# Putting the product of t3 in front of the product of t2 in ten feed-forward pairs of an adaLN + S4 convolution + squared-ReLU kernel

## The chip, the cores and the metric

The kernel runs on one core of a Trainium2 chip. The metric is the device time of one execution in microseconds (us), the median of several runs. Five engines matter here: TensorE (PE in the profile, with its weight loads on a row of their own, PEld), VectorE (DVE), ScalarE (ACT), GpSimd (POOL) and SyncE (SP), which issues nearly all DMAs.

## The reference, cut to what matters

```
mod = (_silu(c) @ w_mod).reshape(c.shape[0], 6, 1, -1)
sa, ca, ga, sb, cb, gb = (mod[:, 0], mod[:, 1], mod[:, 2], mod[:, 3], mod[:, 4], mod[:, 5])
h = _layernorm(x, axis=-1) * (1 + ca) + sa
x = x + ga * _A_ref(h, ...)              # long convolution over 2048 positions, 512 channels
h = _layernorm(x, axis=-1) * (1 + cb) + sb
x = x + gb * _B_ref(h, ...)

def _B_ref(x, w1, b1, w2, b2):           # x 2048 x 512, w1 512 x 1792, w2 1792 x 512
    h = jnp.einsum("bsd,df->bsf", x, w1) + b1
    zero = jnp.zeros_like(h)
    r = jnp.where(h > zero, h, zero)
    h = r * r
    out = jnp.einsum("bsf,fd->bsd", h, w2) + b2
    return out
```

Everything is float32. The change lies in the first product of the feed-forward part, `x @ w1`.

## The kernel before

The first half of the execution (to about 318 us of the span) generates the convolution's kernel and applies it. The feed-forward part fills the rest. It works on the 2048 positions as four blocks of 512, two at a time: `k` is 0 and then 2, and one round computes the blocks `k` and `k + 1`. The 1792 hidden features are 14 tiles of 128, two at a time: a **pair** `j` (0 to 6) makes the tiles `2j` and `2j + 1` for both blocks.

A pair would need eight products of halves (two blocks, two tiles, two halves of the 512 channels). A scheme of the Strassen kind makes them from seven, on sums and differences of the operands. `three(bank, dst, wi, op, start, stop)` is one of them: six matmuls of 128x512 in a row, since weights and operand are each split into a high and a low part (high by high, low by high, high by low, for two groups of 128 channels). `start=True` overwrites the PSUM bank, `start=False` adds to what is in it.

The order of a pair is written out by hand, in `first_half` and `second_half`. From the third pair on (`j` from 2) the banks are `a = tb[0]`, `b = tb[1]`, `c = tb[2]` and `e = tb[3]`; the instruction lists call them ps_163, ps_164, ps_165 and kg_313, and the profile, which leaves numbers out, ps for the first three and kg for the fourth.

1. `"11"` into `a`, overwriting. ScalarE copies `a` to `c0` (line 1184).
2. `"21"` into `b`, overwriting. VectorE adds `b` to `c0` (line 1186). ScalarE and VectorE make the squared ReLU of it (lines 1160, 1165, 1166, 1167), split into high and low, in the buffer t2t.
3. `"t2"` into `a`, **adding**. TensorE may write the bank only once the copy of line 1184 has read it. ScalarE copies the sum to `c1` (line 1194).
4. `"t3"` into `c`, overwriting. VectorE makes `c3 = c1 + c` (line 1196).
5. `"t1"` into `e`, overwriting. VectorE adds `e` to `c3` (line 1198), ScalarE squares it (lines 1160, 1162).
6. 24 matmuls of the second product (`ffn2`, lines 1215 to 1217) for two earlier tiles, into the banks tg. The first twelve take the tile `2j - 1` and the last twelve the tile `2j`, whose squares step 2 has just made.
7. `"t4"` into `c`, adding; VectorE makes `c2 = c1 + c` (line 1203). `"22"` into `e`, adding; VectorE adds it to `c1` (line 1206). Both are squared.

So a pair is 7 x 6 + 24 = 66 matmuls. Between the pairs stand the preparation of weights (`w1_set`: casts on ScalarE and differences on VectorE, lines 1009, 1010 and 1036 to 1039), loads, and on VectorE the residual sums, the statistics of the second normalisation and the output (lines 1113, 1226, 1231, 1244, 1311).

`keep_order` then lays a fixed order on every engine. It plans with costs of its own and a table of numbers, but all matmuls that were put `in_turn` (those of `three` and of `ffn2`) keep the order in which the code issues them. Each engine takes its list strictly in turn, and the waits between engines are semaphores.

Of the kernel before, what the change touches and what calls it, by code (L numbers as in the profile page):

```python
# [358 lines left out]
def tile_adaln_ssm_ffn(  # L359
# [728 lines left out]
    def turn(pe):  # L1088
        in_turn.update(x.ins.name for x in pe)
# [69 lines left out]
    def squares(k, t, c, src=None):  # L1159
        nc.scalar.activation(c, c if src is None else src, AF.Relu, bias=b1c[:, t : t + 1])  # L1160
        if k % 2:
            nc.scalar.activation(rst[:, t], c, AF.Square)
        else:
            h, l = r2_slot(k, t)
            nc.scalar.activation(h, c, AF.Square)
            nc.scalar.activation(c, c, AF.Square)
            nc.vector.tensor_sub(l, c, h.bitcast(F32))  # L1167

    def three(ps, dst, wi, op, start, stop, on=False):
        o = ops[op]  # L1170
        pe = []
        for kt in range(2):
            pe.append(nc.tensor.matmul(  # L1173
                ps, dst[:, 0, wi, kt], o[:, 0, kt], start=start and kt == 0, stop=False, skip_group_check=on))
            pe.append(nc.tensor.matmul(ps, dst[:, 1, wi, kt], o[:, 0, kt], start=False, stop=False, skip_group_check=on))  # L1175
        for kt in range(2):
            pe.append(nc.tensor.matmul(  # L1177
                ps, dst[:, 0, wi, kt], o[:, 1, kt], start=False, stop=stop and kt == 1, skip_group_check=on))
        turn(pe)
# [9 lines left out]
    def second_half(k, j, a, c, e, between):  # L1189
        dst = sets[j % 2]  # L1190
        c1, c2, c3 = quarters(more[:, 0:2048])[1:]
        t = 2 * j
        three(a, dst, 4, "t2", False, True, True)
        nc.scalar.copy(c1, a)
        three(c, dst, 5, "t3", True, True)
        nc.vector.tensor_add(c3, c1, c)
        three(e, dst, 3, "t1", True, True)
        nc.vector.tensor_add(c3, c3, e)  # L1198
        squares(k + 1, t + 1, c3)
        for n in between:  # L1200
            ffn2(k, n, accs)
        three(c, dst, 2, "t4", False, True, True)
        nc.vector.tensor_add(c2, c1, c)
        squares(k, t + 1, c2)
        three(e, dst, 6, "22", False, True, True)
        nc.vector.tensor_add(c1, c1, e)
        squares(k + 1, t, c1)
# [11 lines left out]
    def ffn2(k, t, to):  # L1219
        n = uses.index((k, t))  # L1220
        w2_ready(n + 2)
        product2(k, t, n, to)
# [55 lines left out]
    for k in (0, 2):  # L1278
# [15 lines left out]
        w1_load(2)  # L1294
        w1_load(3)
        second_half(k, 0, tb[0], tb[1], tb[3], [0, 2])
        for _ in w1_set(2, nc.gpsimd):
            pass
        second_half(k, 1, tb[2], tb[1], tb[3], [1])
        for j in range(2, 7):  # L1300
            if j < 6:
                for _ in w1_set(j + 1):
                    pass
            if j < 5:
                w1_load(j + 2)
            if k == 0 and j in (3, 5):
                ss = range(8, 12) if j == 3 else range(12, 16)
                mark = len(nc.cur_bb.bb.instructions)
                for s in ss:
                    nc.sync.dma_start(xos[s % 4], xt[s])  # L1310
                    nc.vector.tensor_add(x2[:, s], x2[:, s], d4(xos[s % 4]))
                    if s % 2:
                        statistics(s - 1)
                hurry(mark, HURRY[55])
            gate_rows(range(4 * k + 2 * j - 4, 4 * k + min(2 * j - 2, 8)))
            first_half(k, j, tb[0], tb[1], cs_[0])
            second_half(k, j, tb[0], tb[2], tb[3], [2 * j - 1, 2 * j])
# [91 lines left out]
```

## Time and profile before

| | us |
|---|---|
| median of 3 runs | 617.12 (617.1 to 618.1) |
| the profiled execution, its own time | 617.67 |
| its span, first to last instruction | 615.9 |
| first changed product in it (first pair with `j = 2`) | 346.51 |
| last matmul starts | 610.13 |
| first and last pair that the change touches, by the copy of line 1184 | 345.9 and 556.3 |

The granted clock of TensorE over the whole span is 0.989 of full speed, and it is 1.00 in every stretch of the feed-forward part that is shown below. In the rows of the timeline the columns are start, duration, engine, line and operation, output and inputs, shape, count, and in brackets the idle time of that engine just before and the instruction that ended it. A matmul's duration overlaps the next one's: what counts is the distance from start to start.

### The profile page before, as it was taken

How to read it: one execution, taken by the hardware profiler on the slowest of the kernel's cores; microseconds unless marked ns; L12 is line 12 of the kernel's file. 1: busy time of each engine (PE TensorE's matmuls, PEld its weight loads, DVE VectorE, ACT ScalarE, POOL GpSimd, SP SyncE). 2: the span in 40 equal slices, each digit the busy share in tenths (PEclk: the TensorE clock that was granted, in tenths of full speed). 3: DMA queues.
4: the chain of work that ended last, by engine and by line, in shares of the span. 5: the costliest groups of instructions: out<-in, count | busy, mean ns of one | idle time of the engine just before them, and what ended most of it. 6: DMA issues, size and time to landing. Idle time of an engine off the chain costs nothing.

```text
span 615.9 us, 21264 instructions
## 1 busy us (share of the span) xinstructions
PE 562.1 (91%) x9238; PEld 484.3 (79%) x9238; DVE 494.9 (80%) x870; ACT 418.6 (68%) x747; POOL 246.7 (40%) x202
## 2 busy tenths in 40 slices
PE   1347998999999999997799999999999999999996
PEld 1235988899899999996677778888888878888885
DVE  6899978999998999945798998547999976654744
ACT  5688869979967678553576866666766766666540
POOL 5549998999998799280004100000000400000000
PEclk9999999999999999998799999999999999999999
DMA  8916041240404401576008131113521532111431
GB/s 307 403 30 202 9 73 31 44 73 4 71 4 72 71 6 27 125 167 224 3 11 278 40 120 35 34 36 99 192 85 55 167 104 69 35 38 40 144 104 69
DMA packets 33133, 57.02 MB, mean 93 GB/s; under 512 B 5520, under 2 KB 14608, under 8 KB 31888
## 3 DMA queue, kind: packets, MB, share of 16 engines
q1 hardware_dynamic: 32752, 55.53, 31.6%
q8 instruction: 72, 1.18, 0.8%
q14 instruction: 21, 0.17, 0.1%
q10 hardware_dynamic: 288, 0.13, 0.1%
HBM read 43.07 MB, written 4.19 MB: 77 GB/s over the span
## 4 chain that ended last, share of the span: by engine, by line
PE 67%; DVE 14%; ACT 9%; issue 4%; DMA 3%; POOL 2%; SPq 1%; DVEq 0%; ACTq 0%; POOLq 0%
PE ps L749 8%; PE ps L903 8%; PE ps L759 7%; PE kg L884 4%; PE ps L1173 4%; PE ps L1175 4%; PE ps L1177 4%; PE tg L1215 3%; PE tg L1217 3%; PE tg L1216 3%; PE tg L1099 2%; PE ps L1217 2%; PE ps L1216 2%; PE ps L1215 2%; DMA work<-w 2%
## 5 line engine op out<-in xcount | busy, mean ns | idle before, releaser
L1036 POOL TENSOR_TENSOR work<-work 128x256 f32<-128x256 f32 x4 | 3.3, 837 | 196.7 <-DVE t2t L1167 134.3
L1010 DVE TENSOR_TENSOR w2t<-rw,w2t 128x512 fp32r<-128x512 f32 x53 | 37.9, 717 | 38.8 <-ACT w2t L1009 38.5
L759 PE MATMUL ps<-xy,t_sb 128*64 128x64 f32 x2048 | 65.9, 223 | 1.0 <-DVE xy L894 1.0
L759 PEld LDWEIGHTS ps<-xy,t_sb 128*64 128x64 f32 x2048 | 63.4, 138 | 2.4 <-DVE xy L894 1.2
L1009 ACT CAST w2t<-rw 128x512 fp32r<-128x512 f32 x53 | 32.8, 619 | 44.6 <-PE kg L1217 21.7
L903 PE MATMUL ps<-e_sb,xy 128*64 128x128 f32 x1024 | 61.0, 274 | 1.9 <-DVE xy L894 1.2
L903 PEld LDWEIGHTS ps<-e_sb,xy 128*64 128x64 f32 x1024 | 56.3, 139 | 3.1 <-DVE xy L894 1.4
L1160 ACT ACTIVATE more<-more,b1c 128x512 f32<-128x512 f32 x54 | 38.9, 720 | 26.4 <-DVE more L1198 15.9
L1215 PE MATMUL tg<-w2t,t2t 128*128 128x512 f32 x112 | 43.9, 392 | 0.5 <-DVE t2t L1167 0.5
L1216 PE MATMUL tg<-w2t,t2t 128*128 128x512 f32 x112 | 43.6, 389 | 0.0
L1217 PE MATMUL tg<-w2t,t2t 128*128 128x512 f32 x112 | 43.6, 389 | 0.0
L894 DVE TENSOR_TENSOR xy<-ps,xy 128x512 f32<-128x512 f32 x64 | 39.9, 681 | 0.5 <-PE ps L759 0.4
L1009 ACT CAST wset<-work 128x512 fp32r<-128x512 f32 (+2 forms) x36 | 24.6, 690 | 22.1 <-DMA work<-w 13.1
L1173 PE MATMUL ps<-opt,wset 128*128 128x512 f32 x84 | 34.1, 405 | 2.4 <-ACT more L1184 2.4
L840 POOL TENSOR_TENSOR llph<-lo,big 128x1024 int32<-128x1024 int32 x16 | 34.3, 2144 | 3.7 <-ACT tg L852 3.6
L840 POOL TENSOR_TENSOR rtlph<-lo,big 128x1024 int32<-128x1024 int32 x16 | 34.4, 2151 | 3.4 <-ACT tg L852 2.8
L749 PE MATMUL ps<-d_sb,ksb 128*64 128x128 f32 x512 | 33.8, 276 | 2.0 <-ACT tg L850 1.4
L1215 PE MATMUL ps<-w2t,t2t 128*128 128x512 f32 x84 | 33.4, 398 | 0.0
L1217 PE MATMUL ps<-w2t,t2t 128*128 128x512 f32 x84 | 32.8, 391 | 0.0
L1175 PE MATMUL ps<-opt,wset 128*128 128x512 f32 x84 | 32.8, 391 | 0.0
L1216 PE MATMUL ps<-w2t,t2t 128*128 128x512 f32 x84 | 32.7, 390 | 0.0
L749 PE MATMUL ps<-d_sb,big 128*64 128x128 f32 x512 | 32.1, 274 | 0.1
(287 smaller groups left out, 1640.1 us busy)
## 6 DMA issues: line engine op xcount, KB each, us to landing
rw<-w SPq DMA_DIRECT2D x53, 256.0 KB, 2.7
xy<-xy SPq DMA_DIRECT2D x64, 128.0 KB, 4.1
xy<-xt SPq DMA_DIRECT2D x24, 256.0 KB, 5.4
work<-w SPq DMA_DIRECT2D x12, 512.0 KB, 4.3
out_dram<-more SPq DMA_DIRECT2D x14, 256.0 KB, 2.2
xy<-w_mod SPq DMA_DIRECT2D x3, 1024.0 KB, 9.9
xy<-w_mod SPq DMA_DIRECT2D x12, 256.0 KB, 3.5
t_sb<-c_t SPq DMA_DIRECT2D x1, 2048.0 KB, 15.3
```

The costliest lines, as they stand in the source:

```text
L749: nc.tensor.matmul(ps[64 * r : 64 * r + 64, 128 * i : 128 * i + 128], src[:, i], d1_sb[:, r], start=True, stop=True)
L759: nc.tensor.matmul(ps[64 * r : 64 * r + 64, 64 * i : 64 * i + 64].rearrange("p (h q t) -> p q h t", h=2, t=2), t2_sb[:, 8 * g + i, r], src ...
L840: nc.gpsimd.tensor_tensor(ph.rearrange("p d r (a b) -> p (d r) a b", a=4), bc(low_phase[:, us].rearrange("p d r b -> p (d r) b"), 2, 4), b ...
L894: nc.vector.tensor_mul(product_piece(y, g), ps, piece(x, g))
L903: nc.tensor.matmul(ps[64 * m : 64 * m + 64, 128 * i : 128 * i + 128], pairs(y)[:, g, i // 2, 64 * m : 64 * m + 64, i % 2], e1_sb[:, h], st ...
L1009: nc.scalar.copy(hi_, raw_)
L1160: nc.scalar.activation(c, c if src is None else src, AF.Relu, bias=b1c[:, t : t + 1])
L1173: pe.append(nc.tensor.matmul(ps, dst[:, 0, wi, kt], o[:, 0, kt], start=start and kt == 0, stop=False, skip_group_check=on))
L1175: pe.append(nc.tensor.matmul(ps, dst[:, 1, wi, kt], o[:, 0, kt], start=False, stop=False, skip_group_check=on))
L1215: nc.tensor.matmul(to[m], l[:, xs], hi_, start=(t == 0), stop=False),
L1216: nc.tensor.matmul(to[m], h[:, xs], lo_, start=False, stop=False),
L1217: nc.tensor.matmul(to[m], h[:, xs], hi_, start=False, stop=(t == NF - 1))])
```

## The change

For `j` from 2 on, in both rounds, the call for t3 stands in front of the call for t2. For `j` 0 and 1 nothing changes (there `c` is another bank or the code before is another).

```
         c1, c2, c3 = quarters(more[:, 0:2048])[1:]
         t = 2 * j
+        if j > 1:
+            three(c, dst, 5, "t3", True, True)
         three(a, dst, 4, "t2", False, True, True)
         nc.scalar.copy(c1, a)
-        three(c, dst, 5, "t3", True, True)
+        if j < 2:
+            three(c, dst, 5, "t3", True, True)
         nc.vector.tensor_add(c3, c1, c)
```

No instruction is added or removed, on any engine. The lines after the edit move down: the copy of line 1194 is line 1196 in the changed kernel, the adds of lines 1196 and 1198 are 1199 and 1201, and the second product's 1215 to 1217 are 1218 to 1220.

The first place is TensorE's list in the first changed pair (`k = 0`, `j = 2`), right behind the product of `"21"`. ps_163 is the bank `a`, ps_165 the bank `c`, opt_5427 the operand t2 and opt_5426 the operand t3. Before:

```order
L1173 MATMUL ps_163<-opt_5427,wset_4635 128x512
L1175 MATMUL ps_163<-opt_5427,wset_4635 128x512
L1173 MATMUL ps_163<-opt_5427,wset_4635 128x512
L1175 MATMUL ps_163<-opt_5427,wset_4635 128x512
L1177 MATMUL ps_163<-opt_5427,wset_4635 128x512 x2
L1173 MATMUL ps_165<-opt_5426,wset_4635 128x512
L1175 MATMUL ps_165<-opt_5426,wset_4635 128x512
L1173 MATMUL ps_165<-opt_5426,wset_4635 128x512
L1175 MATMUL ps_165<-opt_5426,wset_4635 128x512
L1177 MATMUL ps_165<-opt_5426,wset_4635 128x512 x2
```

The same place in the changed kernel:

```order
L1173 MATMUL ps_165<-opt_5426,wset_4635 128x512
L1175 MATMUL ps_165<-opt_5426,wset_4635 128x512
L1173 MATMUL ps_165<-opt_5426,wset_4635 128x512
L1175 MATMUL ps_165<-opt_5426,wset_4635 128x512
L1177 MATMUL ps_165<-opt_5426,wset_4635 128x512 x2
L1173 MATMUL ps_163<-opt_5427,wset_4635 128x512
L1175 MATMUL ps_163<-opt_5427,wset_4635 128x512
L1173 MATMUL ps_163<-opt_5427,wset_4635 128x512
L1175 MATMUL ps_163<-opt_5427,wset_4635 128x512
L1177 MATMUL ps_163<-opt_5427,wset_4635 128x512 x2
```

Six matmuls have changed places with six others; this is so in the ten pairs with `j` from 2 to 6 in both rounds, and nowhere else on TensorE.

The second place is ScalarE's list in the pair `k = 2`, `j = 2`, around the copy of `a` to `c1`. Before:

```order
L1165 ACTIVATE t2t<-more 128x512
L1166 ACTIVATE more<-more 128x512
L1194 COPY more<-ps_163 128x512
L1009 CAST wset_4635<-work 128x512
L1160 ACTIVATE more<-more,b1c 128x512
```

The same place in the changed kernel:

```order
L1165 ACTIVATE t2t<-more 128x512
L1166 ACTIVATE more<-more 128x512
L1009 CAST wset_4635<-work 128x512
L1196 COPY more<-ps_163 128x512
L1160 ACTIVATE more<-more,b1c 128x512
```

The planner has put one cast of the next weights ahead of the copy, in three pairs (`k = 2`, `j` 2, 3 and 4). On VectorE the add of line 1196 changes places with the instruction behind it in four pairs: with the matching subtraction of line 1010 in those three, and with line 1126 in the pair `k = 0`, `j = 6`. The lists of GpSimd and SyncE are the same.

## The prediction

> **What bounds the kernel now.** I read the page first, then the waits of TensorE in the feed-forward part, then the ten places of the edit one by one.
>
> ```profile
> PE 562.1 (91%) x9238; PEld 484.3 (79%) x9238; DVE 494.9 (80%) x870; ACT 418.6 (68%) x747; POOL 246.7 (40%) x202
> ...
> PE 67%; DVE 14%; ACT 9%; issue 4%; DMA 3%; POOL 2%; SPq 1%; DVEq 0%; ACTq 0%; POOLq 0%
> ```
>
> TensorE is busiest and carries 67% of the chain that ended last. In the stretch that holds all ten edited pairs (338 to 573 us), the list of who waited for whom has one wait of TensorE's matmuls, and for its weight loads the same one on top:
>
> ```profile
> PE ps L1173 <- ACT more L1184: 2.4, 3, 1.0
> ...
> PEld ps L1173 <- ACT more L1184: 5.6, 10, 1.5
> ```
>
> Line 1184 is ScalarE's copy of bank `a` to `c0`, line 1173 a product's first matmul. The product that must wait for this copy is t2, and ten weight loads waited: one in each pair that the change touches. Elsewhere TensorE goes from matmul to matmul in these 235 us, so time saved at these ten places moves what follows forward, as long as nobody else is the bound. The busy time by stretch shows who could be:
>
> ```profile
> 348.00:363.00 15.00, 14.21 (x63) 11.48 (x62) 14.72 (x36) 10.47 (x20) 0.00 (x0) 1.00 0.29 89
> 363.00:378.00 15.00, 15.00 (x67) 12.11 (x66) 13.55 (x25) 9.58 (x17) 0.00 (x0) 1.00 0.31 88
> 378.00:393.00 15.00, 15.00 (x67) 12.19 (x66) 9.72 (x16) 10.92 (x19) 0.00 (x0) 1.00 0.13 36
> 423.00:470.00 47.00, 46.99 (x222) 38.66 (x222) 45.79 (x75) 31.48 (x52) 0.00 (x0) 1.00 0.32 101
> ```
>
> The columns are stretch, length, and busy time of PE, PEld, DVE, ACT and POOL, then the granted clock (1.00), the DMA share and GB/s. From 348 to 363 VectorE is busy 14.72 us of 15, more than TensorE; from 378 it has 5 us of air in 15; from 423 to 470, between the rounds, it has 1.2 us in 47. So the pairs with `j` 2 to 4 of the first round are VectorE's as much as TensorE's, and the rest is TensorE's.
>
> **The change, part by part.** First the size of a product and of each stall. The first matmul of t3 and that of t1, one product later:
>
> ```profile
> 348.00 0.39 PE L1173 MATMUL ps<-opt,wset 128*128 128x512 f32 x1
> 349.36 0.39 PE L1173 MATMUL kg<-opt,wset 128*128 128x512 f32 x1
> ```
>
> Six matmuls take 1.36 us, so the step is 0.227 us. The last two matmuls of `"21"` are the row of line 1177 (x2); undisturbed, t2 starts 0.45 us after it and its second matmul (line 1175) 0.68 us after it. What that second matmul is later than this is the loss of the pair:
>
> ```profile
> 345.30 0.61 PE L1177 MATMUL ps<-op,wset 128*128 128x512 f32 x2
> 346.85 0.40 PE L1175 MATMUL ps<-opt,wset 128*128 128x512 f32 x1
> 361.15 0.61 PE L1177 MATMUL ps<-op,wset 128*128 128x512 f32 x2
> 362.89 0.39 PE L1175 MATMUL ps<-opt,wset 128*128 128x512 f32 x1
> 377.19 0.61 PE L1177 MATMUL ps<-op,wset 128*128 128x512 f32 x2
> 378.13 0.40 PE L1175 MATMUL ps<-opt,wset 128*128 128x512 f32 x1
> 392.44 0.61 PE L1177 MATMUL ps<-op,wset 128*128 128x512 f32 x2
> 393.26 0.40 PE L1175 MATMUL ps<-opt,wset 128*128 128x512 f32 x1
> 494.79 0.61 PE L1177 MATMUL ps<-op,wset 128*128 128x512 f32 x2
> 496.43 0.50 PE L1173 MATMUL ps<-opt,wset 128*128 128x512 f32 x1 [1.03 <-ACT more L1184]
> 496.77 0.40 PE L1175 MATMUL ps<-opt,wset 128*128 128x512 f32 x1
> 541.36 0.61 PE L1177 MATMUL ps<-op,wset 128*128 128x512 f32 x2
> 542.18 0.39 PE L1175 MATMUL ps<-opt,wset 128*128 128x512 f32 x1
> ```
>
> The losses are 0.87 (346.85 less 345.30 less 0.68), 1.06, 0.26 and 0.14 us for `j` 2 to 5 of the first round; 1.30 for `j = 2` of the second, and 0.14 for its `j = 5`, with `j` 3 and 4 alike. In the two pairs with `j = 6` I find 0.03 each and leave them out. The sum is 0.87 + 1.06 + 0.26 + 1.30 + 4 x 0.14 = 4.05 us. That is the ceiling of the gain, since the change removes no matmul.
>
> What remains after the swap hangs on when the copy ends. The copies of the four large stalls:
>
> ```profile
> 345.89 0.57 ACT L1184 COPY more<-ps 128x512 f32<-128x512 f32 x1
> 361.93 0.56 ACT L1184 COPY more<-ps 128x512 f32<-128x512 f32 x1
> 377.18 0.57 ACT L1184 COPY more<-ps 128x512 f32<-128x512 f32 x1
> 495.82 0.56 ACT L1184 COPY more<-ps 128x512 f32<-128x512 f32 x1
> ```
>
> They end at 346.46, 362.49, 377.75 and 496.38. In all four the second matmul of t2 follows 0.38 to 0.40 us after the copy's end, so "copy's end plus 0.39" is the earliest for it. After the change its undisturbed place is one product, 1.36 us, later.
>
> - `k = 0`, `j = 2`: place 345.98 + 1.36 = 347.34; earliest 346.85. No stall; gain 0.87.
> - `j = 3`: TensorE arrives 0.87 earlier, place 361.83 - 0.87 + 1.36 = 362.32. The copy will not come earlier: ScalarE waits in this stretch for VectorE, whose list is full. Earliest 362.88, so 0.56 stays. Gain so far 0.87 + 1.06 - 0.56 = 1.37.
> - `j = 4`: place 377.87 - 1.37 + 1.36 = 377.86, earliest 378.14, 0.28 stays against 0.26 now. Gain so far 1.35.
> - `j = 5`: VectorE and ScalarE have air and follow TensorE's pace, so the copy moves forward too; the 0.14 goes. Gain of the first round 1.49.
> - `k = 2`, `j = 2`: place 495.47 + 1.36 = 496.83, earliest 496.77, if the copy moves forward with TensorE: gain 1.30. With `j` 3 to 5 at 0.14 each the second round gains 1.72.
>
> The sum is 1.49 + 1.72 = 3.2 us.
>
> The edit adds no wait to TensorE where t3 now stands. t3 overwrites bank `c`, which the previous pair's add of line 1203 must have read, and its weights come in the same instruction as those of t2:
>
> ```profile
> 343.22 0.68 DVE L1203 TENSOR_TENSOR more<-more,ps 128x512 f32<-128x512 f32 x1
> ...
> 492.53 0.68 DVE L1203 TENSOR_TENSOR more<-more,ps 128x512 f32<-128x512 f32 x1
> ```
>
> These end at 343.90 and 493.21, and t3 would start at 345.75 and 495.24: 1.85 and 2.0 us to spare. I cost this at nothing; its cover is that room.
>
> It does add a wait to ScalarE: the copy of line 1194 can start one product later, and ScalarE's list stands behind it (a cast of weights, then the squaring of `c3`, line 1160). In the tightest pair, and in the second round where the cast now goes first:
>
> ```profile
> 408.01 0.42 PE L1173 MATMUL ps<-opt,wset 128*128 128x512 f32 x1
> ...
> 411.02 0.57 ACT L1194 COPY more<-ps 128x512 f32<-128x512 f32 x1
> ...
> 413.52 0.72 ACT L1160 ACTIVATE more<-more,b1c 128x512 f32<-128x512 f32 x1 [1.94 <-DVE more L1198]
> 500.18 0.62 ACT L1009 CAST wset<-work 128x512 fp32r<-128x512 f32 x1
> ```
>
> In the pair of 411.02 t2 began at 408.01; as second product it ends near 408.01 + 2 x 1.36 + 0.16 = 410.9 (the last matmul lasts 0.39 and not 0.23), still before the copy. Were it late, 1.94 us of idle time behind would take it up. The cast at 500.18 has no idle time before it, so its data had landed, and moving it forward by the copy's 0.5 us costs nothing that TensorE sees. The add of line 1196 needs the copy as it did, and `"t4"`, which adds to its bank, comes only 30 matmuls after t2. The swaps on VectorE move 0.4 to 0.6 us each between neighbours. All at nothing; a bound for each is 0.6 us where its cover is gone.
>
> What comes late next is the second tile's operand in `ffn2`, the low part that VectorE makes in line 1167. Tightest where TensorE leads most and VectorE not yet follows:
>
> ```profile
> 381.95 0.69 DVE L1167 TENSOR_TENSOR t2t<-more,t2t 128x512 fp32r<-128x512 f32 x1 [0.26 <-ACT more L1166]
> 384.73 0.39 PE L1215 MATMUL tg<-w2t,t2t 128*128 128x512 f32 x1
> ```
>
> It ends at 382.64 and is used at 384.73; with a lead of 1.35 at 383.38, which leaves 0.74 us. Enough, but the thinnest margin of all.
>
> A rule of the Trainium skill is to be weighed here. The row is that of 348 to 363: VectorE 14.72, TensorE 14.21. The page "Perfetto Trace Analysis", section "Identifying the Most-Contended Engine", says that the engine with the highest occupancy is the one to improve first, with occupancy a fair measure for VectorE and matmul busy time a bad one for TensorE. By it VectorE is the bound there, and a swap on TensorE's list gives nothing in that stretch. By the rows it is half right: the copy stays where VectorE puts it, yet TensorE needs it one product later.
>
> **Rivals.**
>
> *VectorE holds the lead down.* Its 45.79 us of 47 between the rounds would not follow TensorE, and the copy at 495.82 would stay at its absolute time. Then all that was gained until there counts against one late copy: its earliest place is 496.77, and TensorE behind t2 and t3 is ahead by one product at most, 1.36 us. With 3 x 0.14 behind it, 1.8 us in all. For it: this list, and an output operation that stretches to 2.56 us shortly before that copy. Against: before 423 VectorE has idle time in each pair and starts on what TensorE gives it. By the page of the Trainium skill named above, this case is the one to come.
>
> ```profile
> 488.59 2.56 DVE L1231 TENSOR_TENSOR more<-more,big 128x512 f32<-128x512 f32 x1
> ```
>
> *The wait only moves.* TensorE, early at `ffn2`, waits for line 1167 instead, by as much as it won. That needs the 0.74 us (and more in the other pairs) to vanish and VectorE to lag in both rounds. Gain near nothing.
>
> *Slower: t3 is held by bank `c`.* If VectorE came to the add of line 1203 later than now by over 1.9 us in every pair, each t3 would wait for it in a place that had no wait. At 2.4 us late it is 0.5 us a pair, 5 us in ten, less the 3.2: 1.8 us slower. For it: VectorE's full list in three pairs; against: in the other seven it has the air that 378 to 393 shows, and its order before line 1203 does not change.
>
> That the change does not do what it says is out: TensorE's list has t3 in front in just these ten pairs.
>
> **How the numbers follow.** The sum stands against the profiled execution: 617.67 - 3.2 = 614.5 us. The median of the runs shown (617.12) lies 0.55 below that execution; on the runs' scale I predict 617.12 - 3.2 = 613.9 us. Its own range goes from the ceiling (617.12 - 4.05 = 613.1) to 615.0, where a third is lost: chance 0.70. VectorE holding the lead gives 617.12 - 1.8 = 615.3: 0.17. The wait that only moves gives 617.1: 0.07. Held by bank `c` gives 618.9: 0.06. The range of 8 in 10 is 612.8 to 616.0: the first two cases, with the runs' scatter of some tenths below. What a measurement of this kernel can tell from no change is about 0.2%, 1.23 us, so faster means below 615.9: 0.70 and most of the 0.17, 0.85; within: 0.02 and 0.07, 0.09; slower 0.06.
>
> **What will show it.** In the profile after, TensorE's waits on the copy of line 1184 should be gone in `k = 2`, `j = 2` (1.03 us as recorded) and in `k = 0`, `j = 2`; 0.3 to 0.6 us should stay in `k = 0`, `j` 3 and 4. Weight loads that wait for it should fall from ten to two or three. The distance from the copy at 345.89 to that of the last pair, now 210.4 us (556.3 less 345.9, from the table), should shrink by 3 us, and the last matmul come 3 us earlier. Wrong would be: a new wait of line 1218 on line 1167, of t3 on line 1206 (the old 1203), or a copy at 495.82 that hasn't moved.

## The result, and the profile after

| | before | changed |
|---|---|---|
| median of 20 runs each | 618.13 us (616.44 to 622.8) | 615.31 us (613.0 to 618.05) |
| ratio of changed to before | | 0.9947, 95% interval 0.9935 to 0.9959 |
| span of the profiled execution | 615.9 us | 613.8 us |

The changed kernel is faster by 0.5%; the ratio gives 3.3 us (2.5 to 4.0), the medians 2.8. The forecast was a gain of 3.2 us and a time of 613.9, the range 612.8 to 616.0.

The page of the changed kernel, the row of engines and the chain that ended last, reads almost as before:

```profile
PE 560.4 (91%) x9238; PEld 483.6 (79%) x9238; DVE 495.1 (81%) x870; ACT 419.6 (68%) x747; POOL 247.0 (40%) x202
...
PE 69%; DVE 14%; ACT 8%; issue 3%; POOL 2%; DMA 2%; SPq 1%; DVEq 0%; ACTq 0%; POOLq 0%
```

The waits tell more. Between 338 and 573 us TensorE's matmuls, and below them its weight loads, waited for others as follows (in total, times, longest):

```profile
PE ps L1173 <- ACT more L1184: 0.8, 1, 0.8
PE tg L1218 <- DVE t2t L1167: 0.2, 1, 0.2
...
PEld ps L1173 <- ACT more L1184: 1.6, 2, 1.2
PEld tg L1218 <- DVE t2t L1167: 1.5, 3, 0.6
```

Before, three matmuls waited 2.4 us and ten weight loads 5.6 us for the copy of line 1184; now it is one matmul and two loads. The wait of line 1218 for 0.2 us is the one at 338.28, ahead of the first edited pair, and it was longer before (0.47). The places, in TensorE's timeline of the changed kernel (t2 is now the product behind t3; the releaser is in brackets):

```profile
347.49 0.61 PE L1177 MATMUL ps<-opt,wset 128*128 128x512 f32 x2
347.95 0.39 PE L1173 MATMUL ps<-opt,wset 128*128 128x512 f32 x1
...
363.86 0.50 PE L1173 MATMUL ps<-opt,wset 128*128 128x512 f32 x1 [0.80 <-ACT more L1184]
364.20 0.40 PE L1175 MATMUL ps<-opt,wset 128*128 128x512 f32 x1
...
378.50 0.61 PE L1177 MATMUL ps<-opt,wset 128*128 128x512 f32 x2
379.12 0.50 PE L1173 MATMUL ps<-opt,wset 128*128 128x512 f32 x1
379.47 0.40 PE L1175 MATMUL ps<-opt,wset 128*128 128x512 f32 x1
...
495.95 0.62 PE L1177 MATMUL ps<-opt,wset 128*128 128x512 f32 x2
496.41 0.39 PE L1173 MATMUL ps<-opt,wset 128*128 128x512 f32 x1
```

In `k = 0`, `j = 2` and in `k = 2`, `j = 2` t2 starts 0.46 us behind the last two matmuls of t3: no loss, where 0.87 and 1.30 us were lost before. In `j = 4` the second matmul is 0.97 behind, 0.29 later than the undisturbed 0.68. In `j = 3` 1.07 us is lost (t2's first matmul 0.96 later than the step of 0.227, its second another 0.11). The other six pairs lose nothing.

What that is worth is best read between two points that both kernels share and that lie around the ten pairs: the first matmul of the second product in the pair `k = 0`, `j = 1`, and one behind the last pair of the second round. First the two of before, then the two of the changed kernel:

```profile
337.46 0.50 PE L1215 MATMUL tg<-w2t,t2t 128*128 128x512 f32 x1 [0.47 <-DVE t2t L1167]
...
572.15 0.50 PE L1215 MATMUL tg<-w2t,t2t 128*128 128x512 f32 x1
```

```profile
338.28 0.50 PE L1218 MATMUL tg<-w2t,t2t 128*128 128x512 f32 x1 [0.18 <-DVE t2t L1167]
...
570.03 0.50 PE L1218 MATMUL tg<-w2t,t2t 128*128 128x512 f32 x1
```

Before, TensorE needs 234.69 us for the distance, now 231.75: **2.94 us less**. The spans differ by only 2.1, because this execution came to the first point 0.82 us later, in work that the edit does not touch. From here on "the distance" is this number, and "lost at t2" is the sum over the ten pairs. (The expectations below call the distance "from the first to the second round's start"; it begins in the first round and ends behind the second.)

### The profile page after: what moved, and what is told of

Same layout as the page of the kernel before. It is cut to its first block, busy times and chain, and to the rows that moved or that the text cites. A ratio compares the mean times of both kernels' runs of the same rounds, so it can differ in the third digit from the quotient of the medians.

```text
span 613.8 us, 21258 instructions
## 1 busy us (share of the span) xinstructions
PE 560.4 (91%) x9238; PEld 483.6 (79%) x9238; DVE 495.1 (81%) x870; ACT 419.6 (68%) x747; POOL 247.0 (40%) x202
## 4 chain that ended last, share of the span: by engine, by line
PE 69%; DVE 14%; ACT 8%; issue 3%; POOL 2%; DMA 2%; SPq 1%; DVEq 0%; ACTq 0%; POOLq 0%
PE ps L903 7%; PE ps L749 7%; PE ps L759 6%; PE ps L1173 4%; PE ps L1175 4%; PE ps L1177 4%; PE tg L1218 4%; PE tg L1220 4%; PE tg L1219 4%; PE kg L884 3%; PE ps L1220 3%; PE ps L1218 3%; PE ps L1219 3%; PE kg L1173 2%; PE kg L1175 2%
```

## The experiments

There were ten runs. In all of them the same instructions are issued; what differs is an order. The planner lays the lists anew each time, so a run that moves something by hand also differs in some places of the lists of ScalarE and VectorE, all of them behind 343 us. In "swap in the first pair alone" the lists of ScalarE, VectorE and GpSimd are those of before, and in the repeats those of the run repeated. Their profiles, beside those of before and of the changed kernel (the last two columns: the time of before in the runs taken with it, and the ratio to it):

| kernel | lost at t2, us | the distance, us | time, us (runs) | before, us | ratio |
|---|---|---|---|---|---|
| before | 4.05 | 234.69 | 618.13 (20) | | |
| changed | 1.36 | 231.75 | 615.31 (20) | 618.13 | 0.9947 (0.9935 to 0.9959) |
| changed, second profile | 0.72 | 231.08 | 614.94 (7) | 618.22 | 0.9932 (0.9907 to 0.9958) |
| changed, third profile | 1.04 | 231.46 | 615.16 (1) | 617.54 | |
| swap in the first pair alone | 4.0 | 234.69 | 618.69 (1) | 618.71 | |
| swap in `k = 2`, `j = 2` alone | 3.0 | 233.62 | 616.27 (1) | 618.71 | |
| t3, t1, then t2 | 0 | 230.60 | 614.03 (6) | 618.71 | 0.9937 (0.9914 to 0.9959) |
| the same, second profile | 0 | 230.60 | 613.78 (12) | 618.22 | 0.9928 (0.9907 to 0.9949) |
| t3 already between "11" and "21" | 0.37, and 0.23 at t3 | 231.66 | 614.47 (5) | 618.71 | 0.9936 (0.9913 to 0.9960) |
| changed, one cast put behind the copy | 0.89 | 231.26 | 614.66 (7) | 618.22 | 0.9926 (0.9899 to 0.9953) |
| before, copy ahead of the squarings | 2.16 | 232.60 | 616.24 (12) | 618.22 | 0.9971 (0.9952 to 0.9990) |
| before, copy ahead of both ReLUs | 0 | 230.36 | 613.10 (6) | 617.54 | 0.9930 (0.9913 to 0.9947) |

**One swap alone, where VectorE's list is full.** The forecast says that the copy in `j = 3` does not come earlier when TensorE does, so a lead won in `j = 2` is lost one pair later. (Not shown here and in the next two runs: the `if` in front of the later call for t3 is changed to match, in the third also one in front of the call for t1.)

```
-        if j > 1:
+        if k == 0 and j == 2:
             three(c, dst, 5, "t3", True, True)
```

> Only the pair k = 0, j = 2 has t3 in front; the other nine stay as before. My theory (in the next pair, j = 3, the copy of bank a is late because VectorE and a load of second weights make it late, not because TensorE is): the stall of 0.87 us at j = 2 goes, but the whole lead is lost at j = 3, whose stall of t2 grows from 1.06 to about 1.9 us (up to 2.4 if the load is as late as in the changed kernel's profile); from j = 4 on nothing is gained, 0 to 0.1 us. Rival (the copy follows TensorE): the stall at j = 3 stays at 1.06 and 0.87 us are gained.

The first loss went, and the next one grew:

```profile
363.64 0.50 PE L1173 MATMUL ps<-opt,wset 128*128 128x512 f32 x1 [1.72 <-ACT more L1184]
```

It is 1.99 us now (1.89 to the first matmul, 0.10 more to the second) where before lost 1.06, so 0.93 came back of the 0.87 won. The copy had not moved: it starts 24.52 us behind the first point, where it started 24.47 behind it before. The distance is 234.69 us, as before. So in these pairs a lead is worth only what the next copy's place allows, and the swap in `j = 3` is what keeps the gain of the one in `j = 2`.

**One swap alone, where VectorE has air.**

```
-        if j > 1:
+        if k == 2 and j == 2:
```

> Only the pair k = 2, j = 2 has t3 in front. My theory: its stall of 1.30 us goes whole, nothing gives it back later, and TensorE's stalls at t2 in the first round are as before (0.87, 1.06, 0.26, 0.14). Counted from the first ffn2 matmul of the second round to the last matmul the kernel is 1.3 us shorter. Rival (the wait only moves): TensorE waits by about as much, 1 us, for the second tile's operand of ffn2 in that pair or the next, and the gain is under 0.3 us.

The loss of 1.30 us in that pair went. The distance can be divided at the matmul that stands in the first round where the second point stands in the second (423.21 before, 423.11 here). Up to it nothing was won: 86.00 us where before took 85.75, since t2 in `j = 3` lost 1.24 instead of 1.06. From there to the second point it took 147.62 us where before took 148.94: 1.32 less. The whole of the 1.30 was kept.

**t2 as the third product.** Two products between "21" and t2, so that the copy has 1.36 us more.

```
-        if j > 1:
+        late = j > 1
+        if late:
             three(c, dst, 5, "t3", True, True)
+            three(e, dst, 3, "t1", True, True)
         three(a, dst, 4, "t2", False, True, True)
```

> In the ten pairs the order is t3, t1, t2, so t2 has two products of room behind the product of 21 and the adds to c3 come after both. My theory: the stalls left in the changed kernel at k = 0, j = 3 and 4 (1.07 and 0.29 us) go too, and the gain over the kernel before is 3.7 to 4.1 us (ratio 0.9933 to 0.9940); what may come up is a wait of ffn2's second tile on the low part of the squares at k = 0, j = 4, 0.1 to 0.5 us, where TensorE now leads by 2.2 us and the room was 2.1. Rival (VectorE is the bound in that stretch): the 1.4 us come back as such waits, and the ratio is that of the changed kernel, 0.9947. Second rival: the copy of c1, two products later now, holds up ScalarE's list and the gain is smaller than the changed kernel's.

No loss at t2 is left. In its place is the thinnest margin of the forecast, line 1167 against the second tile of the second product in `k = 0`, `j = 4` (line 1167's rows of VectorE carry the same number in this kernel, the second product's lines are 1221 to 1223):

```profile
381.53 0.69 DVE L1167 TENSOR_TENSOR t2t<-more,t2t 128x512 fp32r<-128x512 f32 x1 [0.27 <-ACT more L1166]
```

```profile
381.91 0.39 PE L1223 MATMUL tg<-w2t,t2t 128*128 128x512 f32 x1
382.27 0.50 PE L1221 MATMUL tg<-w2t,t2t 128*128 128x512 f32 x1
382.61 0.40 PE L1222 MATMUL tg<-w2t,t2t 128*128 128x512 f32 x1
```

The subtraction ends at 382.22 and the matmul follows at 382.27: 0.25 us lost up to the matmul behind it. So the wait that only moves exists, but it is small, and in this pair it begins only when TensorE has won more than the swap wins. The gain was within the forecast (a ratio of 0.9937, forecast 0.9933 to 0.9940).

**t3 one product earlier.** This takes 1.36 us from the 1.85 that t3 had to spare for bank `c`. (Not shown: the call for t3 in `second_half` goes for these pairs, and `tb[2]` is handed over as `c`.)

```
     three(a, dst, 0, "11", True, True)
     nc.scalar.copy(c0, a)
+    if c is not None:
+        three(c, dst, 5, "t3", True, True)
     three(b, dst, 1, "21", True, True)
```

> In the ten pairs the order is 11, t3, 21, t2, t1: t2 keeps the place that it has in the changed kernel, t3 goes one product earlier still and 21 one later. My theory: the stalls at t2 are those of the changed kernel; bank c, whose room was 1.85 to 2.0 us in the changed kernel, still has about 0.5 us and holds t3 nowhere or by at most 0.3 us a pair; the squares of c0 come one product later, so ffn2's second tile waits for them by about 0.6 us at k = 0, j = 4. Ratio 0.9947 to 0.9965. Rival of the prediction (t3 is held by bank c): t3's first matmul waits for VectorE's add of c2 in most pairs, by 0.3 us or more, and the kernel is no faster than before.

One t3 was held. In `k = 0`, `j = 4` its second matmul starts 0.91 us behind the last two of "11" where 0.68 is undisturbed, so 0.23 us is lost: VectorE's add that reads bank `c` (line 1206 in this kernel) ends only at 376.14.

```profile
375.62 0.61 PE L1177 MATMUL ps<-op,wset 128*128 128x512 f32 x2
376.19 0.50 PE L1173 MATMUL ps<-opt,wset 128*128 128x512 f32 x1
376.53 0.40 PE L1175 MATMUL ps<-opt,wset 128*128 128x512 f32 x1
...
375.46 0.68 DVE L1206 TENSOR_TENSOR more<-more,ps 128x512 f32<-128x512 f32 x1
```

The other nine were not held, so the rival, 0.3 us or more in most pairs, did not come; with 1.36 us less room the bank begins to matter in one pair. t2 lost 0.37 us in `j = 3`. The second product waited for line 1167, 0.55 us, in `k = 2`, `j = 2` and not in `k = 0`, `j = 4` as forecast. The ratio, 0.9936, is better than the 0.9947 to 0.9965 forecast. Here the planner also moved instructions of ScalarE and VectorE and one load of SyncE, so the 231.66 us is not the price of this move alone.

**The load in front of the copy.** In `j = 3` the changed kernel lost 1.07 us where 0.56 was forecast. ScalarE's list there, with the waits in brackets:

```profile
359.83 0.62 ACT L1009 CAST w2t<-rw 128x512 fp32r<-128x512 f32 x1 [1.10 <-DMA rw<-w]
360.36 0.40 ACT L1009 CAST wset<-work 128x256 fp32r<-128x256 f32 x1
360.67 0.72 ACT L1160 ACTIVATE more<-more,b1c 128x512 f32<-128x512 f32 x1
...
363.24 0.57 ACT L1184 COPY more<-ps 128x512 f32<-128x512 f32 x1
```

From the cast of a weight of the second product to the copy ScalarE has no idle time, and the cast waited for its load. The ReLU of line 1160 could have started when VectorE's add of line 1206 was done, at 359.91:

```profile
359.23 0.68 DVE L1206 TENSOR_TENSOR more<-more,ps 128x512 f32<-128x512 f32 x1
```

So the cast was put behind the copy, with this addition to the planner:

```
+    group_of = {i.name: g for g, il in enumerate(groups) for i in il}
+    for x, y in links:
+        before[group_of[y]].add(group_of[x])
...
+[(copied[0, 3], cast_of[7])]
```

> The changed kernel with one thing more: in the pair k = 0, j = 3 ScalarE's cast of a second-product weight (w2t from rw), which in the changed kernel stood three squarings and two casts ahead of the copy of bank a and waited 1.10 us for its load, is put behind that copy. TensorE's list is that of the changed kernel. Theory: the 1.07 us left at t2 in this pair is set by that load, since ScalarE takes its list in turn. Without it the squaring ahead of the copy waits only for VectorE's add, which ended at 359.91 in the changed kernel where the squaring started at 360.67: the copy comes about 0.7 us earlier and 0.3 to 0.4 us is left of 1.07. From the first to the second round's start TensorE needs 231.1 instead of 231.75 us, and the time is 0.4 to 0.7 us below that of the changed kernel. Rival: VectorE sets the copy (14.7 us busy of 15 there), the load only ended the wait last by a little; then 0.8 to 1.1 us stays at t2 and the time is that of the changed kernel.

> The changed kernel once more, for the spread between executions: from the first to the second round's start 231.2 to 232.0 us (231.75 in its first profile), with 0.5 to 1.1 us left at t2 of k = 0, j = 3, by when the load ahead of the copy lands. If the 1.07 us were fixed by VectorE's list it would come out at 1.0 to 1.1 again.

> The changed kernel a third time, one look: what is left at t2 of k = 0, j = 3 follows the landing of the load that ScalarE's cast ahead of the copy needs (1.07 us left where the cast started 0.60 after VectorE's add began, 0.44 where it started 0.16 after it); 231.0 to 231.8 us between the starts of the rounds.

With the cast gone, the ReLU waits for VectorE, and the copy comes 3.29 us after that add's start where it came 4.01 after it (its lines are 6 higher, the add is line 1212, start 359.37):

```profile
360.08 0.73 ACT L1166 ACTIVATE more<-more,b1c 128x512 f32<-128x512 f32 x1 [0.91 <-DVE more L1212]
...
362.66 0.57 ACT L1190 COPY more<-ps 128x512 f32<-128x512 f32 x1
```

0.37 us is left in `j = 3`, as forecast, but 0.52 in `j = 4`: counted from the first point, TensorE came there 0.70 us earlier than in the first profile of the changed kernel and the copy only 0.46 earlier, so 0.2 is given back. The distance, 231.26 us (forecast 231.1), lies within what the changed kernel itself took (231.08 to 231.75), and the times can't tell the two kernels apart either (614.66 and 614.94 on one chip). So this run shows what sets the copy, but no gain. The repeats of the changed kernel say more: the cast, the copy and the same add of VectorE in the second profile, then in the third:

```profile
357.82 0.62 ACT L1009 CAST w2t<-rw 128x512 fp32r<-128x512 f32 x1 [0.66 <-DMA rw<-w]
...
361.23 0.56 ACT L1184 COPY more<-ps 128x512 f32<-128x512 f32 x1
...
357.66 0.68 DVE L1206 TENSOR_TENSOR more<-more,ps 128x512 f32<-128x512 f32 x1
```

```profile
359.19 0.62 ACT L1009 CAST w2t<-rw 128x512 fp32r<-128x512 f32 x1 [0.90 <-DMA rw<-w]
...
362.59 0.56 ACT L1184 COPY more<-ps 128x512 f32<-128x512 f32 x1
...
358.79 0.68 DVE L1206 TENSOR_TENSOR more<-more,ps 128x512 f32<-128x512 f32 x1
```

In all three profiles the copy starts 3.40 or 3.41 us after the cast. After the start of VectorE's add the cast came by 0.16, 0.40 and 0.60 us (second, third and first profile), and 0.44, 0.80 and 1.07 us were lost at t2. Counted from the first point of each execution (in the same order), the add came at 20.78, 20.93 and 20.95 us and the cast at 20.94, 21.33 and 21.55, so the cast moved by 0.61 us, as the loss did (0.63), and the add by 0.17. The load was issued at 17.94, 18.09 and 18.11 and landed 2.9, 3.2 and 3.4 us later. The loss follows the landing of the load: the same lists lose more or less from one execution to the next. Why the load takes longer or shorter is not shown. The second profile's 231.08 us and 0.44 lie just below the 231.2 to 232.0 and 0.5 to 1.1 forecast for it, the third within its range.

**The copy moved instead of the product.** If the wait is the cost, and not the order of products, then TensorE's order of before must do as well once ScalarE copies earlier. Line 1184's copy needs only the product of "11", but it stood behind the previous pair's ReLUs and squarings. First it was put ahead of the squarings:

```
+        links.append((copied, squared[k, 2 * j - 1]))
```

> The kernel before (t2 in front of t3), with ScalarE's list changed instead of TensorE's: the planner must put the copy of bank a (c0) ahead of the two squarings of the previous pair's c2 (lines 1165 and 1166, 0.53 and 0.54 us apart), and rearranges VectorE's, ScalarE's and SyncE's lists around it. Theory: the loss at t2 is the wait for this copy and nothing in the order of products itself, so it goes without the swap: the stalls of 1.30 (k = 2, j = 2) and of the four times 0.14 us go, those of k = 0 shrink; 2 to 3.5 us gained, 614.5 to 616 us. Rival: what the copy gains is given back, since the squares of c2, 1.1 us earlier in the list before, now come late for the second product (line 1215 on line 1167) or VectorE, which is full there, becomes later: the stalls at t2 go, new waits of the second product come, and the time is 617 to 619.

Half of it went: 0.77, 0.11 and 0.48 us are lost in `j` 2 to 4 of the first round and 0.80 in `k = 2`, `j = 2`, where the forecast had the whole 1.30 gone; the time, 616.24, just misses the 614.5 to 616 forecast. The copy was still behind the ReLU of `c1`, and that waits for VectorE's add of the product "22" (line 1213 here):

```profile
347.46 0.72 ACT L1165 ACTIVATE more<-more,b1c 128x512 f32<-128x512 f32 x1 [0.53 <-DVE more L1213]
348.09 0.56 ACT L1189 COPY more<-ps 128x512 f32<-128x512 f32 x1
```

Then it was put ahead of both ReLUs:

```
+        links.extend((copied, relus[x]) for x in ((k, 2 * j - 1), (k + 1, 2 * j - 2)))
```

> The kernel before (t2 in front of t3) with the copy of bank a put ahead of both ReLUs of the previous pair (of c2 and of c1, line 1160), not only ahead of the squarings as in the last try, where it still stood behind the ReLU of c1. ScalarE's copy then needs nothing but the end of the product of "11", which comes about 2.8 us ahead of the second matmul of t2. Theory: the cost is the copy's place in ScalarE's list; all ten losses at t2 go (4.05 us) without any change of TensorE's order, at most 0.5 us of it comes back at the second product (its squares are one copy, about 0.5 us, later); 230.4 to 231.2 us from the first to the second round's start where the kernel before has 234.69, and 3.4 to 4.2 us less time. Rival: losses at t2 go, but the later squares make TensorE wait in the second product (line 1215 on line 1167) or at the next "21" and more than 1.5 us of it come back.

In all ten pairs the copy now waits for TensorE, here in the first pair and in `k = 2`, `j = 2`:

```profile
343.51 0.59 ACT L1189 COPY more<-ps 128x512 f32<-128x512 f32 x1 [1.24 <-PE ps L1182]
...
490.61 0.59 ACT L1189 COPY more<-ps 128x512 f32<-128x512 f32 x1 [0.30 <-PE ps L1182]
```

All ten losses are gone, with t2 in its old place. In the ten pairs neither a matmul nor a weight load waits for the later squares; three weight loads wait 1.4 us for line 1172 (the old 1167), at the first point, between the rounds and at the second point, where those of before and of the changed kernel wait too. The distance, 230.36 us, and the gain in time, 4.4 us, come out slightly better than forecast. Its windows, in the columns of the prediction:

```profile
348.00:363.00 15.00, 15.00 (x68) 12.42 (x67) 14.79 (x34) 11.11 (x21) 0.00 (x0) 1.00 0.30 79
423.00:470.00 47.00, 47.00 (x223) 38.80 (x223) 46.41 (x74) 31.26 (x50) 0.00 (x0) 1.00 0.32 102
```

TensorE is busy 15.00 us of 15 beside a VectorE at 14.79. At 613.10 us this is the fastest kernel measured here, though its interval overlaps those of the changed kernel and of "t3, t1, then t2".

**t2 as the third product, once more.**

> t3, t1 and then t2, once more and on the same chip as the changed kernel. Theory: every loss at t2 is gone here (230.6 us from the first to the second round's start, 1.15 less than in the changed kernel's first profile), so it is about 1 us below the changed kernel's time. Rival: what it wins beyond the changed kernel is within the spread between executions, and the two times agree within 0.5 us.

The distance was 230.60 us again, 0.48 less than the changed kernel's profile on the same chip. Its time was 613.78 us against 614.94 for the changed kernel, 1.2 us less, but the two intervals of the ratio overlap almost wholly, so the times alone don't show it; and about 0.3 of the 1.2 lies outside the span, as the last section says.

## Why the prediction was right

*What bounds the kernel.* Right: the ten places carried the gain. The distance less what is lost at t2 is 230.4 to 230.7 us in eleven of the twelve profiles of the table, whichever way the loss was removed, and 231.3 with t3 between "11" and "21", where 0.23 us was lost at t3 and 0.55 at the second product instead. Matmul by matmul in the second round, the lead of the changed kernel over before grows by 1.35, 0.18, 0.17, 0.18 and 0.06 us in the five pairs and by nothing between them. So each stall cost a little more than its second matmul shows (1.30, 0.14 three times, 0.03), and the ceiling of 4.05 was a little low: the copy ahead of both ReLUs won 4.33.

*The pairs one by one.* Of the 4.05 us, 0.84 was forecast to stay, in `j` 3 and 4. In `j = 4` 0.28 was forecast and 0.29, 0.28 and 0.24 measured. In `j = 3` 0.56 was forecast and 1.07, 0.44 and 0.80 measured, 0.77 in the mean. This is the mis-sized term. The step behind it read "The copy will not come earlier: ScalarE waits in this stretch for VectorE", and took the copy's time from one execution. VectorE is only one of the two for which ScalarE's list waits there; the other is the load of a weight, and it moves the copy by some tenths from one execution to the next. With the cast out of the way VectorE alone left 0.37; the rest is the load. The trace of before had shown it too, as the idle time of ScalarE's cast at 358.53:

```profile
358.53 0.62 ACT L1009 CAST w2t<-rw 128x512 fp32r<-128x512 f32 x1 [0.64 <-DMA rw<-w]
```

*The two rounds.* Forecast were 1.49 and 1.72 us. The three profiles of the changed kernel gained 1.03, 1.69 and 1.31 in the first round, and 1.91, 1.92 and 1.92 in the second (147.02 or 147.03 us where before took 148.94). Both together are 3.26 us in the mean of the three; 3.2 was forecast. That they agree so closely is in part luck: the first round came out 0.15 below its forecast in the mean, by the load, and the second 0.20 above it, by stalls that cost more than was read. The kernel before has only one profile; in the first round, "swap in `k = 2`, `j = 2` alone" has its order and took 0.25 us longer, so the gains of the first round are no surer than that.

*The earliest place of t2.* "Copy's end plus 0.39" held in every pair that was stalled at t2, in all profiles: 363.81 and 364.20 in the changed kernel, 361.79 and 362.18 in its second profile, 348.65 and 349.04 with the copy ahead of the squarings.

*The rival "VectorE holds the lead down".* It fell. Between the rounds VectorE moved with TensorE, at 45.85 us of 47 where it had 45.79:

```profile
423.00:470.00 47.00, 47.00 (x222) 38.81 (x223) 45.85 (x74) 31.57 (x52) 0.00 (x0) 1.00 0.32 101
```

and the copy of `k = 2`, `j = 2` (495.82 before, 495.50 after) came 1.14 us earlier as counted from each execution's first point. What the prediction drew for 348 to 363 from the rule of the Trainium skill's page "Perfetto Trace Analysis", section "Identifying the Most-Contended Engine", no gain since VectorE is the busier engine, did not come: with the copy ahead of both ReLUs the stretch lost its stalls at a VectorE busier still (14.79). What decided each loss was when one copy came. In one sense it was half right, as the prediction has it: with the swap in `j = 2` alone, the lead was lost to a copy that did not move. But there too ScalarE's list waited last for the load (its cast at 359.62 waited 0.68 us for it), not for VectorE.

*The wait that only moves.* Not in the changed kernel. It showed at 0.25 us in "t3, t1, then t2", in the pair that the forecast called the tightest, and as 0.55 us in `k = 2`, `j = 2` with t3 between "11" and "21".

*Held by bank `c`.* It fell in the changed kernel. With 1.36 us less room one t3 of ten was held, by 0.23 us.

*The signs that were named.* Weight loads that wait for the copy fell from ten to two; the first and last copies lie 207.5 us apart and not 210.4 (forecast: 3 less), by the line of the copy in the changed kernel:

```profile
L1184 ACT COPY more<-ps x12: 566/567/591, 346.7 to 554.2; 128x512 f32<-128x512 f32 x12
```

The last matmul came only 2.1 us earlier (608.03 against 610.13), since this execution was 0.82 us late at the first point; that sign mixed the change with the scatter of the first half.

*The time.* 613.9 us came from three runs of before (617.12); twenty gave 618.13. On that scale the same gain gives 614.9, against 615.31 measured. Most of the difference lies outside the span: there the changed kernel takes about 0.3 us more, as the last section says.

## What to carry to other kernels

When an in-order engine waits for a small copy, look at what stands ahead of the copy in the copying engine's list, not at how long the copy takes: here moving the copy past two ReLUs, with what the planner rearranged around it, was worth all ten stalls, and moving the waiting product back was worth three quarters of them. A stall removed pays only if the next wait of the same kind moves too, so walk the lead through the places one after another before adding up the gains. And where a term is the time of one instruction, ask what else its list waits for: a load there makes the term a spread.

## What the runs showed that was not expected

Most of the scatter between executions lay ahead of the feed-forward pairs. The first point came between 336.38 and 339.73 us in the twelve profiles, though the lists of ScalarE, VectorE and GpSimd up to it are the same, while the second point and the last matmul were 37.98 us apart in the kernel before and 38.00 in all three profiles of the changed one. So two executions are better compared over the distance than over the span.

A run's time is longer than the span of its instructions, and not by the same amount in every kernel: by 1.74 to 1.85 us in the 48 runs of before that were taken beside the experiments, by 1.67 to 1.91 in the other experiments, and by 2.06 to 2.18 in all 28 runs of the changed kernel. So about 0.3 us of what the swap wins within the span is lost outside it, which fits the medians' 2.8 us beside the 2.9 to 3.6 of the distance. Why is not known.
